# Seven products for the last first product: attention and a two-layer network on one Trainium2 core

## The chip, the cores and the metric

One core of a Trainium2 chip runs the whole program. The metric is the device time of one launch in microseconds (us). The kernel before takes 290.84 us, the median of three runs (290.55 to 291.35).

## The reference

Eight batches of eight heads, 576 tokens, 64 columns a head. Each token attends to the tokens at most 32 places from it. The result, all heads of a token side by side (4608 tokens of 512 columns), goes through two matrix products with the square of ReLU between them.

```python
scores = scale * np.matmul(q, k.transpose(0, 1, 3, 2))
mask = np.abs(pos[:, None] - pos[None, :]) <= window
attn = softmax(np.where(mask, scores, -1e9))
x = np.matmul(attn, v).transpose(0, 2, 1, 3).reshape(B * S, H * D)
h = x @ w_in
r = np.maximum(h, 0.0)
return (r * r) @ w_out
```

`w_in` is 512 x 2048 and `w_out` 2048 x 512. All matrix products take bf16 and add up in f32.

## The kernel before, in words

**Units and groups.** The tokens are counted in units of 64, 72 in all. Attention goes by groups G of 192 tokens (24 of them). For a group: POOL issues the loads of q, k and v, which turn f32 into bf16 on the way (`load_qk`, L469; `load_v`, L517); SP issues DMA transposes of q and k (`turn_dma`, L603; the first six groups are turned on PE by `turn_pe`, L555); PE makes the scores (`S6B` is that of group 6), ACT takes the exponent (`X`), DVE multiplies by the mask (`M`), PE multiplies by v (`P6A`, `P6B`, L753), DVE takes the reciprocal (`R`) and writes the normalised rows into XA and XB (`N`), and SP turns these by DMA into XT (`T6a`, `T6b`, L854 and L857). The first groups (G under NXT) are turned on PE instead, into a bank of `at`, and ACT copies them to XT (L833, L838, L850).

**First product** (`mm1`, L862). `A3840.4` is the product of the tile that starts at token 3840 and of hidden blocks 4 and 5 (128 columns each): four matmuls a block, over the four quarters of 512 columns, into a bank `ht`. ACT takes the ReLU (`r`), ACT or DVE the square (`g`), into the ring GT. Tiles have 192 tokens up to token 2304 and 256 from there (TILES).

**Second product** (`mm2_pair`, L935). Two blocks of 128 tokens (pair u, u + 1) are taken together, as a 2 x 2 block product by seven products instead of eight (Winograd's form of Strassen's): DVE makes four sums S of GT (L951), each of `P1.u` to `P7.u` is eight matmuls of 256 columns on PE (L965), two products to a bank, and ACT and DVE add up the banks: a copy `p1`, the sums `u2`, `u4` and `c22` of 256 columns, `cc` of 512 and a last copy `c11`. The combinations TW of `w_out` are made once (`setup_tw`). The first two blocks go the plain way (`mm2`, `B0.0`). From pair ULATE on, every other pair takes the attention's banks in `at` and other buffers. ACT issues the stores (`st`).

**What sets the order.** Every step is recorded with its engine, what it reads and writes, a planned duration and a key: the place in units at which it is wanted. `schedule` (L168) plays the program through with these numbers and gives each engine, whenever it is free, the ready step with the least key. OFFS moves the keys of ACT's and DVE's steps by kind, FLEX lets some steps go to ACT or DVE, whichever is free, at a handicap, and NOISE moves every key by a draw from SEEDS. What comes out is a fixed order for each engine; each engine then works through its own in turn, and waits on semaphores by bank or buffer. The keys: attention of group G at 3 G - LEAD, a tile of the first product at its place in units, pair u at 2 u + LAGP, so LAGP is the lag of the second product behind the first. Loads wait for a gate: the second v product of the group GD before theirs.

Of the kernel before, what the change touches and what calls it, by code (L numbers as in the profile page):

```python
# [6 lines left out]
ALU = mybir.AluOpType  # L7
# [14 lines left out]
TG = 6  # L22
NXT = 3
# [6 lines left out]
GK = 8.0  # L30
TDKEY = 6
XKEY = (0.2, 0.5)
QMOVE = 14.8
HMOVE = 27
# [5 lines left out]
TGAP = 28  # L40
NVR = 24
VKEY = 10.0
TSLACK = 3500
XSLACK = 2500
LSLACK = 3000
# [19 lines left out]
TILES = ((192, 2304), (256, 4608))  # L65
SEEDS = (54889, 73113, 37345, 76131, 20885, 97248, 47624, 10448, 1997, 7471, 50773, 3305, 47783, 64133, 39018, 28670, 69087, 23028, 92194, 70005)
NOISE = 0.0
NBIAS = 1
PKEY = 2
# [12 lines left out]
LAGP = 8.0  # L82
PSTEP = 0.4
SLEAD = 2.5
MOE = -1
SQBEG = 768
ULATE = 28
HLATE = 4352
E3 = 576
E3B = 1  # L90
OFFS = {'S': 3.25, 'M': -1.5, 'g': 2.25, 'Z': -3.5, 'N': 2.75, 'cc.': -4.25, 'u': -2.75, 'X': 3.25, 'r': -2.25, 'c': -2.25}
DLEAD = 0.3
TWKEY = 6
# [3 lines left out]
FLEX = {'g': 5.25, 'Z': 4.75, 'ev': 3.0, 'o': 6, 'p': 0.75}  # L97
# [259 lines left out]
class Gen:  # L357
# [105 lines left out]

    def gate(self, G):
        if G < 6:
            return None
        return self.p.named[GATE.format(G - GD)] if G >= GFAR else self.moe

    def load_qk(self, t, b, g, key):  # L469
# [6 lines left out]
        for j in range(2):  # L476
            self.p.rec("POOL", lambda e, j=j: e.dma_start(raw[0:h, j, :].rearrange("p (h d) -> p h d", h=8), s[:, j]),  # L477
                       writes=[("raw", t, G % NRAW, j)], dma=(f"{t}{G % NRAW}{j}", G), key=key, dur=500 + 3 * h,
                       move=(h // 2, QMOVE), name=f"{t}{b}{g}{j}", after=self.gate(3 * b + g), slack=LSLACK if b > 1 else 0)
# [22 lines left out]
    def load_pair(self, t, b, g, key):  # L502
# [11 lines left out]
                   reads=[("pr", t, G % NPR)], writes=[("raw", t, G % NRAW, x) for x in range(2)], key=3 * G - LEAD - PKEY if b == 0 else key, dur=430,  # L514
                   name=f"c{t}{b}{g}")

    def load_v(self, b, g, key, js=(0, 1)):  # L517
        G = 3 * b + g
        vt = self.V[G % NV]
        for j in js:  # L520
            k0 = 192 * g - 32 + 128 * j
            lo, hi = max(k0, 0), min(k0 + 128, S_)
            if g and j == 0 and G < NVR:
# [4 lines left out]
                writes=[("v", G % NV, j)], dma=(f"v{G % NV}{j}", G), key=key, dur=500 + 3 * n, move=(n // 2, VMOVE),  # L528
# [89 lines left out]
    def scores(self, G, ws):  # L618
# [3 lines left out]
        key = 3 * G - LEAD + 0.3 * ws[0]  # L622
# [60 lines left out]
    def scores_steps(self, G):  # L683
# [3 lines left out]
        key = 3 * G - LEAD  # L687
# [41 lines left out]
    def pv(self, G, w):  # L729
        b, g = divmod(G, 3)  # L730
        n = 2 * G + w
        key = 3 * G - LEAD + 0.3 * w + 0.1
# [56 lines left out]
    def xturn(self, G):  # L789
        xa, xb = self.XA[G % 3], self.XB[G % 3]  # L790
        key = 3 * G - LEAD + 0.5
        r = 192 * G % RING
        wr = [("xt", (3 * G + c) % (RING // 64)) for c in range(3)]
        if G < NXT:
            ps = self.AT[:, 1024:1536].bitcast(BF16)
            bank = self.half(2)
# [65 lines left out]
    def mm1(self, t0, n, ds, key):  # L862
# [26 lines left out]
        if SQBEG <= t0 < SQEND and k % SQMOD[1] in SQMOD[0]:  # L889
# [6 lines left out]
                   if "g" in FLEX else None)  # L896

# [160 lines left out]
    def build(self):  # L1058
# [40 lines left out]
        for G in range(NG):  # L1099
            b, g = divmod(G, 3)  # L1100
            if b > 1:
                key = 3 * G - LEAD - (GK if G >= GFAR else AHEAD)
# [9 lines left out]
            for ws in ((0,), (1,)) if G < NSPLIT else ():  # L1112
                at(3 * G - LEAD + 0.3 * ws[0], self.scores, G, ws)
# [67 lines left out]
```

## Time and profile before

| | |
|---|---|
| median of the runs | 290.84 us |
| profiled execution, whole | 292.3 us |
| its span, first to last instruction | 290.1 us |
| TensorE's granted clock, mean | 0.999 |
| read from HBM, written | 36.70 MB, 9.44 MB |
| DMA packets | 160645, of which 149984 under 512 B |

The profiled execution spends 2.2 us outside the span and lies 1.5 us above the median. In the tables, PE is TensorE's matmuls, PEld its weight loads, DVE VectorE, ACT ScalarE, POOL GpSimd; a row of a group gives its count, busy time, mean length of one in ns, and the idle time of the engine ahead of it with what ended that. In the stretches, the number after an engine's name is its busy time in that stretch. In the timeline a row has start, length, engine, line and operation. A matmul's recorded length overlaps that of the next one.

### The profile page before, as it was taken

Reading aid. Unit: us, or ns where it says so; the run is one execution under the profiler, and the core shown is the slowest. Engines: PE = TensorE matmul, PEld = TensorE weight load, DVE = VectorE, ACT = ScalarE, POOL = GpSimd, SP = SyncE. Lnnn points to the kernel's source line nnn. Section 1 sums busy time; section 2 is a strip of 40 time slices with the busy share of each in tenths; the row PEclk is TensorE's granted clock in tenths of the full one; section 3 lists DMA queues with packets and bytes.
Section 4 is the critical chain, followed back from the end, with each engine's and each line's share of the span. In section 5 each row is a group of like instructions: output and inputs, shape, how many; then the busy total and the mean of one; then the engine's idle time right before and its main releaser. Section 6 shows DMA issues by size and latency. Waiting matters only on the chain.

```text
span 290.1 us, 8378 instructions
## 1 busy us (share of the span) xinstructions
PE 283.0 (98%) x3426; PEld 245.6 (85%) x3430; DVE 208.2 (72%) x451; ACT 206.3 (71%) x379; POOL 107.0 (37%) x143
## 2 busy tenths in 40 slices
PE   7988999999999999999999999999999999999996
PEld 2467885889999999999998898888888888988885
DVE  6668779878687878686968886766876877735263
ACT  3379987586989988778776677758687638688520
POOL 8986660141566066326415435606236000000000
PEclk9999999999999999999999999999999999999999
DMA  9999999999999999999999999999999921202024
GB/s 161 188 194 186 197 178 139 200 135 173 113 143 209 129 165 119 173 171 143 124 150 189 150 127 169 131 190 90 169 106 139 143 91 29 84 18 76 0 75 145
DMA packets 160645, 39.97 MB, mean 138 GB/s; under 512 B 149984, under 2 KB 156256, under 8 KB 160608
## 3 DMA queue, kind: packets, MB, share of 16 engines
q0 software_dynamic: 106016, 17.93, 94.2%
q1 hardware_dynamic: 49552, 12.47, 31.4%
q10 hardware_dynamic: 5040, 9.05, 9.8%
q8 instruction: 27, 0.44, 0.7%
q14 instruction: 10, 0.08, 0.1%
HBM read 36.70 MB, written 9.44 MB: 159 GB/s over the span
## 4 chain that ended last, share of the span: by engine, by line
PE 87%; DVE 6%; ACT 3%; DMA 1%; issue 1%; ACTq 0%; DVEq 0%
PE ht L879 39%; PE outp L965 29%; PE at L965 4%; PE at L753 4%; PE at L697 3%; PE outp L405 2%; DMA oe<-in_q_dram 1%; PE at L879 1%; PE outp L905 1%; PE outp L879 1%; DVE xa L775 1%; DVE tw L932 1%; ACT qt L596 1%; DVE kt L599 1%; ACT e L674 1%
## 5 line engine op out<-in xcount | busy, mean ns | idle before, releaser
L879 PE MATMUL ht<-xt,w 128*128 128x192 bf16 (+1 forms) x1248 | 135.9, 258 | 0.0
L879 PEld LDWEIGHTS ht<-xt,w 128*128 128x128 bf16 x1248 | 109.3, 98 | 7.9 <-ACT qt L596 0.3
L885 ACT ACTIVATE rt<-ht 128x384 bf16<-128x384 f32 (+1 forms) x156 | 82.4, 534 | 36.4 <-PE ht L879 31.4
L477 POOL DMA_DIRECT2D kraw<-in_k_dram x36 | 27.7, 775 | 113.1 <-PE at L753 54.6
L895 ACT ACTIVATE gt<-rt 128x384 bf16<-128x384 bf16 (+1 forms) x116 | 65.3, 569 | 4.4 <-ACT rt L885 1.5
L526 POOL DMA_DIRECT2D v<-in_v_dram x48 | 37.7, 793 | 0.0
L965 PE MATMUL outp<-w,gt 128*128 128x256 bf16 x240 | 31.1, 273 | 0.0
L965 PE MATMUL outp<-tw,gt 128*128 128x256 bf16 x240 | 31.1, 273 | 0.0
L965 PE MATMUL outp<-tw,ss 128*128 128x256 bf16 x240 | 30.5, 273 | 0.3 <-DVE ss L951 0.2
L893 DVE TENSOR_TENSOR gt<-rt 128x384 bf16<-128x384 bf16 (+1 forms) x52 | 19.9, 386 | 13.5 <-ACT rt L885 13.0
L477 POOL DMA_DIRECT2D qraw<-in_q_dram x36 | 27.7, 773 | 0.0
L711 ACT ACTIVATE e<-at 128x1024 bf16<-128x1024 f32 x21 | 21.4, 1020 | 7.3 <-PE at L697 7.0
L965 PEld LDWEIGHTS outp<-tw,ss 128*128 128x128 bf16 x240 | 22.9, 98 | 3.1 <-issue 0.3
L965 PEld LDWEIGHTS outp<-w,gt 128*128 128x128 bf16 x240 | 23.0, 98 | 3.0 <-ACT oe L915 0.5
L965 PEld LDWEIGHTS outp<-tw,gt 128*128 128x128 bf16 x240 | 22.9, 98 | 2.5
L985 DVE TENSOR_TENSOR oe<-outp,uu 128x256 f32<-128x256 f32 (+1 forms) x30 | 16.6, 554 | 8.2 <-ACT rt L885 4.9
L719 DVE TENSOR_TENSOR pt<-e,mask 128x1024 bf16<-128x1024 bf16 x21 | 14.5, 691 | 11.1 <-ACT e L711 11.0
L753 PE MATMUL at<-v,pt 128*128 128x66 bf16 x384 | 20.1, 194 | 0.1
L753 PEld LDWEIGHTS at<-v,pt 128*128 128x128 bf16 x384 | 17.8, 98 | 2.2 <-ACT at L783 0.4
L725 DVE TENSOR_TENSOR pt<-em,mask 64x512 bf16<-64x512 bf16 x42 | 17.6, 420 | 1.7 <-ACT em L714 0.3
L775 DVE TENSOR_TENSOR xa<-at,rs 64x512 bf16<-64x512 f32 x24 | 16.7, 695 | 1.1
L775 DVE TENSOR_TENSOR xb<-at,rs 128x512 bf16<-128x512 f32 x24 | 16.5, 686 | 0.8
(112 smaller groups left out, 321.8 us busy)
## 6 DMA issues: line engine op xcount, KB each, us to landing
out_dram<-oe ACTq DMA_DIRECT2D x34, 256.0 KB, 4.0
qraw<-in_q_dram POOLq DMA_DIRECT2D x36, 96.0 KB, 6.2
w<-in_moe_w_in_dram POOLq DMA_DIRECT2D x4, 512.0 KB, 11.1
v<-in_v_dram POOLq DMA_DIRECT2D x16, 128.0 KB, 7.8
w<-in_moe_w_out_dram POOLq DMA_DIRECT2D x4, 512.0 KB, 17.7
v<-in_v_dram POOLq DMA_DIRECT2D x16, 96.0 KB, 7.0
kraw<-in_k_dram POOLq DMA_DIRECT2D x12, 112.0 KB, 5.5
kraw<-in_k_dram POOLq DMA_DIRECT2D x12, 96.0 KB, 4.4
```

The costliest lines, as they stand in the source:

```text
L477: self.p.rec("POOL", lambda e, j=j: e.dma_start(raw[0:h, j, :].rearrange("p (h d) -> p h d", h=8), s[:, j]), writes=[("raw", t, G % NRAW, ...
L526: self.p.rec("POOL", lambda e, j=j, lo=lo, hi=hi, k0=k0: e.dma_start(vt[lo - k0:hi - k0, j, :, 0:64], self.v[b, :, lo:hi, :].rearrange("h ...
L711: self.p.rec("ACT", lambda e: e.activation(e2[:], self.AT[:, 0:1024], ACTF.Exp, scale=0.125), reads=lo, writes=[("e", n)], key=key, dur=ac ...
L725: self.p.rec("DVE", lambda e, w=w, r=r, x=x, mm=mm: e.tensor_tensor(pt[x:x + 64, w, :, 0:64], e1[r:r + 64, :].rearrange("p (h q) -> p h q" ...
L753: mm = e.matmul(avp[:, c:c + VS], pt[:, 4 * (h % 2) + h // 2, :], vt[:, w, h, :], start=(w == 0 and y == 0), stop=True, skip_group_check=True)
L775: self.p.rec("DVE", lambda e: e.tensor_tensor(x[r0:128, :].rearrange("p (x y c) -> p x y c", x=2, y=4), av[:, :, :, 0:64], rb, ALU.mult), ...
L879: mm = e.matmul(ht[:, n * x:n * x + n], self.W1[:, ft, 128 * d:128 * d + 128], self.XT[:, ft, r:r + n], start=(ft == 0), stop=(ft == 3))
L885: self.p.rec("ACT", lambda e: e.activation(rt[:, 0:c], ht[:, 0:c], ACTF.Relu), reads=htag, writes=[("rt", k % 4)], key=key, dur=act(c), na ...
L893: self.p.rec("DVE", lambda e: e.tensor_tensor(gt[:, d0:d0 + len(ds), r:r + n], rr, rr, ALU.mult), reads=[("rt", k % 4)], writes=wr, key=ke ...
L895: alt=("ACT", lambda e: e.activation(gt[:, d0:d0 + len(ds), r:r + n], rr, ACTF.Square), act(c), "g")
L965: mm = e.matmul(op[:, 256 * half:256 * half + 256], a[:, d, :], w[:, d, :], start=first and d == 0, stop=d == 7, skip_group_check=True)
L985: self.p.rec("DVE", lambda e: e.tensor_tensor(out, src, other, ALU.add), reads=btags[bank] + rd, writes=wr, key=key + k * PSTEP - DLEAD, d ...
```

## The change

**The first product of the last 512 tokens.** Tokens 4096 to 4607 are one tile (STR1), a 2 x 2 block product by seven products: halves of the hidden width, of the 512 columns, and of the tokens. `setup_w1s` makes four combinations of `w_in` (eight DVE steps of 1024 columns, `ws`) in buffers of q and k that the last groups no longer need. `mm1_tile` makes four differences of XT (`t`, 512 columns each, on DVE). `mm1_pair` is called for dd = 0 to 7 and does hidden blocks dd and dd + 8 for all 512 tokens: four PE steps `a` to `d` of 4, 4, 2 and 4 matmuls of 256 columns into two banks, a copy `p1` and a ReLU of 256 columns on ACT, sums `u2`, `u4`, `c22` (256 columns) and `cc` (512) on DVE, a maximum over 768 columns (DVE or ACT) and a square over 1024 (DVE or ACT). Even dd use the banks `ht`, odd dd two of `at`.

**The numbers.** Tiles of 192 tokens go on to token 3072. NXT goes from 3 to 5, so groups 3 and 4 are turned on PE. Attention's key falls by 0.2 a group from group 6 on (`pos`), so a group takes 2.8 units. The lag of the second product is 9 and grows by 0.2 for each block past the eighth, to 14.2. Loads from group 12 on are gated one group earlier. Planned times of late loads and transposes, OFFS, FLEX, NOISE and SEEDS change, and with them the order of nearly everything.

```diff
-NXT = 3
+NXT = 5
-GK = 8.0
+GK = 7.0
+LAGS = 0.2
+GDL = 1
-TSLACK = 3500
-XSLACK = 2500
-LSLACK = 3000
+TSLACK = 2200
+XSLACK = 3000
+LSLACK = 2000
+STR1 = (4096,)
+LG0 = 6
+LGS = 0.2
+WLEAD = 5.0
-TILES = ((192, 2304), (256, 4608))
+TILES = ((192, 3072), (256, 4608))
-NOISE = 0.0
+NOISE = 0.4
-LAGP = 8.0
+LAGP = 9
-SLEAD = 2.5
+SLEAD = 1.0
-ULATE = 28
-HLATE = 4352
+ULATE = 26
+HLATE = 3840
...
+    def pos(self, G):
+        return 3 * G - LEAD - max(0, G - LG0) * LGS
...
-        return self.p.named[GATE.format(G - GD)] if G >= GFAR else self.moe
+        return self.p.named[GATE.format(G - GD - GDL * (G > LG0))] if G >= GFAR else self.moe
...
+    def mm1_pair(self, t0, dd, key):
...
+        banks = [(self.HT[0][:], self.HT[1][:]), (self.AT[:, 1024:1536], self.AT[:, 1536:2048])][i]
...
+        L = [w(0, lo), w(1, lo), ws(3), w(1, hi), ws(0), ws(1), ws(2)]
+        R = [B[0, 0], B[1, 0], B[1, 1], T[3], T[0], T[1], T[2]]
...
+        prod((0, 5), 0, (0, 1), True, 0, "a")
+        prod((4, 6), 1, (0, 1), True, 1, "b")
...
+        add(u2, al[:, 256:512], p1, btags[0] + tp1[:1], tu2, 1, 256, f"u2.{t0}.{dd}")
+        add(u4, be[:, 0:256], u2, btags[1] + tu2[:1], tu4, 2, 256, f"u4.{t0}.{dd}")
+        add(rh[:, 768:1024], be[:, 256:512], u4, btags[1] + tu4[:1], rtag[2], 3, 256, f"c22.{t0}.{dd}")
+        prod((1,), 0, (0,), False, 4, "c")
...
+        prod((2, 3), 1, (0, 1), False, 5, "d")
...
-            key = 2 * u + LAGP - 4 * (u == NBLK - 2)
+            key = 2 * u + LAGP + LAGS * max(0, u - 8) - 4 * (u == NBLK - 2)
```

**The order, at two places.** First PE around the start of the second product, some 45 to 55 us into the run. In the kernel before, from the last parts of B1 and B0 (L905) to P1, P5 and P7 of pair 2 (L965) and the first tile past 576 tokens (L879):

```order
L905 MATMUL outp<-w,gt 128x512 x4
L753 MATMUL at<-v,pt 128x66 x8
L905 MATMUL outp<-w,gt 128x512 x4
L965 MATMUL outp<-w,gt 128x256 x8
L965 MATMUL outp<-tw,ss 128x256 x8
L965 MATMUL outp<-tw,gt 128x256 x8
L879 MATMUL ht<-xt,w 128x192 x16
```

In the changed kernel the same place, where L891 is the first product, L1025 `B`, L1085 `P`, L765 the v product of group 4, and L845 and L850 its turn on PE:

```order
L891 MATMUL ht<-xt,w 128x192 x16
L765 MATMUL at<-v,pt 128x66 x8
L1025 MATMUL outp<-w,gt 128x512 x4
L891 MATMUL ht<-xt,w 128x192 x16
L1025 MATMUL outp<-w,gt 128x512 x4
L765 MATMUL at<-v,pt 128x66 x8
L1025 MATMUL outp<-w,gt 128x512 x8
L1085 MATMUL outp<-w,gt 128x256 x8
L845 MATMUL at<-ident,xa 128x64 x4
L850 MATMUL at<-ident,xb 128x128 x4
L1085 MATMUL outp<-tw,ss 128x256 x16
```

The eight steps of tile 576 (A576) moved from behind P1 of pair 2 to ahead of it, and the turn of group 4 came in.

Then the end of the tile of seven products. On PE of the changed kernel (L968 is `mm1_pair`): P6, P5 and P7 of pair 30, the two operands of A4096.7d, P2, P3 and P4 of pair 30, and P1 of pairs 32 and 34:

```order
L1085 MATMUL at<-tw,qraw 128x256 x16
L1085 MATMUL at<-tw,gt 128x256 x8
L968 MATMUL at<-xt,kraw 128x256 x2
L968 MATMUL at<-qt,w 128x256 x2
L1085 MATMUL at<-w,gt 128x256 x8
L1085 MATMUL at<-w,qraw 128x256 x8
L1085 MATMUL at<-tw,gt 128x256 x8
L1085 MATMUL outp<-w,gt 128x256 x8
L1085 MATMUL at<-w,gt 128x256 x8
```

On DVE of the changed kernel, the same place: c22.4096.7 (into v3), u2.30, the square of dd = 6, cc.4096.7, u4.30 and c22.30, then the first S of pairs 34 and 32 (L1071):

```order
L995 TENSOR_TENSOR v3<-at,v1 128x256
L1105 TENSOR_TENSOR e1<-at,e0 128x256
L1014 TENSOR_TENSOR gt<-v2 128x2x512
L995 TENSOR_TENSOR v3<-at,v0 128x512
L1105 TENSOR_TENSOR em0<-at,e1 128x256
L1105 TENSOR_TENSOR oe<-at,em0 128x256
L1071 TENSOR_TENSOR qraw0<-gt 128x1024
L1071 TENSOR_TENSOR ss<-gt 128x1024
```

In the kernel before, A4352.14, the last step of its first product, has the fourteen products of pairs 32 and 34 behind it; here A4096.7d, the last of the new one, has three products of pair 30 and these fourteen behind it, and u4.30 and c22.30 stand behind cc.4096.7 on DVE.

More of the change, by code (lines that the diff above doesn't have):

```diff
@@ L29 @@
 GD = 3
-GK = 8.0
-TDKEY = 6
+GK = 7.0
+TDKEY = 5.0
 XKEY = (0.2, 0.5)
 QMOVE = 14.8
+QM2 = 21.4
+TBK = 0
+LAGS = 0.2
+KPL = 0
+GDL = 1
 HMOVE = 27
@@ L794, in xturn @@
         if G < NXT:
-            ps = self.AT[:, 1024:1536].bitcast(BF16)
-            bank = self.half(2)
+            ps = (self.OUTP[0][:] if 0 < G < TBK else self.AT[:, 1024:1536]).bitcast(BF16)
+            bank = ["outp0"] if 0 < G < TBK else self.half(2)
             two = G < NBIAS
```

141 lines of the change are left out of this document (120 added, 21 removed), and 4 rows, old and new, of the table OPENING.

## Prediction

> **What bounds the kernel now.** First the page, for the span, the busy shares and the chain that ended last.
>
> ```profile
> span 290.1 us, 8378 instructions
> PE 283.0 (98%) x3426; PEld 245.6 (85%) x3430; DVE 208.2 (72%) x451; ACT 206.3 (71%) x379; POOL 107.0 (37%) x143
> PE 87%; DVE 6%; ACT 3%; DMA 1%; issue 1%; ACTq 0%; DVEq 0%
> ```
>
> The chain of work that ended last runs through PE for 87%. The page does not say where the other 13% lies, so next comes the busy time of each engine by stretches, cut where the work changes.
>
> ```profile
> core 0: us, PE busy (x) PEld busy (x) DVE busy (x) ACT busy (x) POOL busy (x), PEclk, DMA share, GB/s
> 0.00:20.00 20.00, 17.34 (x148) 8.89 (x150) 13.17 (x47) 8.98 (x12) 17.67 (x27) 1.00 1.35 179
> 20.00:40.00 20.00, 18.95 (x288) 17.44 (x288) 15.24 (x33) 19.65 (x40) 12.56 (x17) 1.00 1.64 188
> 40.00:75.00 35.00, 34.48 (x430) 27.98 (x430) 29.43 (x62) 25.25 (x49) 11.16 (x16) 1.00 1.78 160
> 75.00:196.00 121.00, 120.92 (x1582) 110.45 (x1581) 91.77 (x190) 93.73 (x181) 51.79 (x68) 1.00 1.71 154
> 196.00:260.00 64.00, 64.00 (x740) 56.56 (x738) 45.01 (x96) 46.08 (x79) 13.84 (x18) 1.00 0.92 98
> 260.00:287.40 27.40, 27.34 (x251) 24.26 (x248) 13.19 (x25) 12.58 (x23) 0.00 (x0) 1.00 0.16 59
> ```
>
> From 75 us to 287.4 us PE is never idle, at a granted clock of 1.00, while DVE and ACT leave a fifth to a half of their time. There only the sum of PE's own work can shorten the kernel. Before 40 us ACT is full (19.65 of 20 us), so work put on ACT there is paid for. After 260 us DVE has 14 us to spare and ACT 15 us: this is the cover that the change draws on.
>
> A busy sum counts pipelined matmuls more than once, so PE's work is priced from start to start. These are two steps of the chain in order of time (16 matmuls of 192 tokens, 16 of 256) and the group of one product by shape.
>
> ```profile
> 130.86 1.32 PE ht L879 x16
> 257.64 1.75 PE ht L879 x16
> L965 PE MATMUL outp<-w,gt 128*128 128x256 bf16 x240 | 31.1, 273 | 0.0
> ```
>
> A matmul of 256 columns takes 1.75/16 = 0.109 us of PE, one of 192 takes 0.0825 us; a product of eight takes 0.87 us. The group's own mean, 273 ns, is two and a half times that. [...] By the mean, 16 matmuls fewer would be 4.4 us; by the steps, which I use, 1.75 us.
>
> **The change part by part.** *PE's own work.* The first product of the last 512 tokens took 16 hidden blocks x 4 x 2 = 128 matmuls of 256 columns and takes 7 products x 2 x 8 = 112: -16 x 0.109 = -1.75 us. Then NXT sends the turns of groups 3 and 4 to PE. PE's rows where group 1 is turned price that:
>
> ```profile
> 26.58 0.29 PE L833 MATMUL at<-ident,xa 64*128 64x64 bf16 x4 [0.61 <-DVE xb L775]
> 26.80 0.40 PE L838 MATMUL at<-ident,xb 128*128 128x128 bf16 x4
> 27.03 0.82 PE L879 MATMUL ht<-xt,w 128*128 128x192 bf16 x8
> ```
>
> From 26.58 to 27.03 is 0.45 us a group: +0.90 us. TILES takes 768 tokens from tiles of 256 to tiles of 192: 256 x 0.0825 - 192 x 0.109 = 21.1 - 20.9 = +0.2 us. PE's sum: -1.75 + 0.90 + 0.2 = -0.65 us. No other edit touches the number of matmuls.
>
> *The waits of PE that the new order can take away.* PE's rows between 45 and 75 us show two, each with a neighbour that starts on time:
>
> ```profile
> 50.91 1.05 PE L965 MATMUL outp<-w,gt 128*128 128x256 bf16 x8
> 52.05 1.03 PE L965 MATMUL outp<-tw,ss 128*128 128x256 bf16 x8
> 62.51 0.42 PE L753 MATMUL at<-v,pt 128*128 128x66 bf16 x8
> 62.76 1.03 PE L965 MATMUL outp<-tw,gt 128*128 128x256 bf16 x8
> 64.64 0.41 PE L753 MATMUL at<-v,pt 128*128 128x66 bf16 x8
> 65.28 1.05 PE L965 MATMUL outp<-tw,ss 128*128 128x256 bf16 x8 [0.22 <-DVE ss L951]
> ```
>
> P1 of pair 2 takes 1.14 us to the next start instead of 0.87 (DVE is still making TW), and the step at 64.64 takes 0.64 us where the one at 62.51 takes 0.25 (S of pair 4 is late): 0.27 + 0.39 = 0.66 us. In the new order a whole tile of 192 tokens (A576, eight groups of 0.66 us) comes ahead of P1 of pair 2, and pair 4 starts a tile later. I take both waits as gone, -0.65 us; the bounds are 0 and, if the 0.61 us wait in the row at 26.58 goes as well, -1.3 us. That one I expect to stay: the turn of group 1 still stands behind the same mask, reciprocal and XB on DVE. What comes next where these go is PE's queue itself.
>
> *ACT before 45 us.* XT of groups 3 and 4 adds two evictions on ACT, and two of K's evictions move there from DVE, against two squares and a clearing that move off; from 20 to 40 us there is no cover. By the rows below (0.81 us an XT) the bounds are 0 and +1.0 us; I take 0, since the XTs come after 40 us, where ACT has 10 of 35 us free, and what is added and removed before that differs by less than one of them. With the turns go four transposes of SP's queue; at that place no wait of PE is for one of them, so nothing is gained.
>
> *The last stretch, DVE.* These are groups by shape: DVE's reads of 256 and 512 columns of PSUM, S, square, copy, then ACT's.
>
> ```profile
> L985 DVE TENSOR_TENSOR uu<-outp,uu 128x256 f32<-128x256 f32 x30 | 12.6, 421 | 3.1 <-ACT uu L976 1.5 <-PE outp L965 0.5
> L985 DVE TENSOR_TENSOR oe<-outp,uu 128x512 f32<-128x512 f32 x15 | 10.4, 691 | 8.0 <-ACT rt L885 4.9 <-PE outp L965 2.9
> L951 DVE TENSOR_TENSOR ss<-gt 128x1024 bf16<-128x1024 bf16 x15 | 10.3, 689 | 3.0 <-ACT gt L895 2.4 <-PE outp L965 0.2
> L893 DVE TENSOR_TENSOR gt<-rt 128x512 bf16<-128x512 bf16 x24 | 10.1, 424 | 7.6 <-ACT rt L885 7.3
> L512 DVE COPY qraw<-tw 96x1024 bf16<-96x1024 bf16 x5 | 2.4, 472 | 0.1
> L711 ACT ACTIVATE e<-at 128x1024 bf16<-128x1024 f32 x21 | 21.4, 1020 | 7.3 <-PE at L697 7.0
> L850 ACT ACTIVATE xt<-at 128x768 bf16<-128x768 bf16 x2 | 1.6, 811 | 0.1
> ```
>
> From A4096.0a to the end of A4096.7d PE has 112 x 0.109 + 15 products x 0.87 = 25.3 us of work. DVE's queue over the same stretch (u2.26 to cc.4096.7) holds 31 sums of 256 columns, 10 of 512, 3 S, 3 squares of 1024 and 2 maxima: 31 x 0.42 + 10 x 0.69 + 6 x 0.69 + 2 x 0.47 = 25.0 us. The maximum over 768 columns of bf16 has no row; the copy of 1024 (0.47) is nearest, bounds 0.42 and 0.69. [...] Either way DVE, which had up to half its time free here, is as full as PE, and what it has left over for waiting is 0.3 us. Its four t and eight ws (1.7 and 5.5 us) come earlier, the ws spread over the middle of the run, where a quarter of DVE is free: nothing.
>
> Where that shows is the end of the stretch. How long DVE takes to see a product:
>
> ```profile
> 270.58 1.04 PE L965 MATMUL at<-w,gt 128*128 128x256 bf16 x8
> 271.66 0.42 DVE L978 COPY oe<-at 128x256 f32<-128x256 f32 x1 [0.79 <-PE at L965]
> ```
>
> 270.58 + 0.87 is 271.45, and DVE starts 0.2 us later. With T the end of A4096.7d: cc.4096.7 ends at T + 0.2 + 0.69, u4.30 and c22.30 behind it in DVE's queue end at T + 1.73. P3.30 needs c22.30; PE has only P2.30 (0.87 us) until then, and waits 0.86 us. Nothing had to wait there before. The square of the last pair (0.81 + 1.02 us on ACT after cc) ends at T + 2.72, ahead of P1.32 at T + 3.5, and the S of pairs 32 and 34 fit beside the 14 products left: no second wait. I take +0.86 us, bounds +0.6 us (each of the three sums starts some 0.1 us before the one ahead has ended) and +3.0 us (the hand-offs between ACT, DVE and PE inside the eight units add two more waits of 1 us, since DVE cannot catch up).
>
> *Loads.* These are PE's scores of groups 6, 10 and 23, then the turns of XB (time to landing, and one issue of them) and the PE step that needs that one:
>
> ```profile
> 67.13 0.23 PE L697 MATMUL at<-qt,kt 64*128 64x64 bf16 x4
> 103.28 0.41 PE L697 MATMUL at<-qt,kt 64*128 64x64 bf16 x16
> 244.28 0.41 PE L697 MATMUL at<-qt,kt 64*128 64x64 bf16 x16
> DMA to landing us min/median/max: 2.4/6.3/8.3
> 84.00 2.03 SPq L857 DMA_TRANSPOSE xt<-xb  x1
> 94.83 1.43 PE ht L879 x16
> ```
>
> A group comes every 9.0 us at first (36.2/4) and every 10.8 us after (141/13). The new keys put 2.8 units between groups instead of 3, which is about 10.1 us: loads and turns come closer, but not closer than they stood early on, where the turn issued at 84.00 lands by 92.3 at the longest, 2.5 us ahead of its reader. At the end T23b has 13 products (11.3 us) between P23B and A4096.0a; reciprocal, u2, XB, turn and t take 0.2 + 0.2 + 0.42 + 0.69 + 6.3 + 0.42 = 8.2 us. I take 0, bounds 0 and +2 us.
>
> *Sum*: -0.65 - 0.65 + 0.86 = -0.44 us. The profiled execution took 292.3 us, 2.2 us outside its span of 290.1; nothing outside the span is changed. It lies 1.5 us over the median of 290.84, so the difference goes to the median: **290.4 us**. A measurement of this kernel tells 0.3%, 0.87 us, from no change.
>
> **The rivals.** *DVE sets the last 40 us (slower).* The eight units pass each sum from ACT to DVE to PE, one bank at a time. For it: 25.0 of 25.3 us, and every wait of DVE stays. Against it: sums that do not depend on each other start before the one ahead has ended, so 25.0 is high. With waits of 3.0 us, 290.84 - 1.30 + 3.0 = 292.5 us; from 2.2 us on the kernel is slower by over 0.3%. [...] Chance 0.15.
>
> *A turn lands late (slower).* XT of one group comes after its first product is due, and PE, in order, waits. For it: denser groups, and two turns of K and Q between XA and XB in SP's queue. Against it: the margin of 2.5 us at 9 us a group, and loads gated one group earlier. A turn 4 us later than the longest here costs 4 - 2.5 = 1.5 us: 291.9 us; it decides from 3.8 us on. Chance 0.08.
>
> *The small early waits go too (faster).* PE stood idle for 20 - 18.95 = 1.05 us from 20 to 40 us (0.61 of it in the row at 26.58) and for 0.5 us from 40 to 75; the whole order is drawn anew there, with a larger lag and so with more first products at hand when something is late. Against it: ACT is full from 20 to 40 us and gets no less to do. 290.4 - 1.05 = 289.35 us; with the other 0.5 us 288.9. Chance 0.30.
>
> *The gain is not made (no change).* XT and K on ACT before 45 us take what the order gives: 290.84 - 0.65 + 0.86 = 291.05 us or some tenths less. Chance 0.07.
>
> **How the numbers follow.** The forecast case (289.8 to 291.0) has 0.40; 0.07 of it lies under 289.97. Faster: 0.30 + 0.07 = 0.37. Same: 0.33 + 0.07 = 0.40. Slower: 0.15 + 0.08 = 0.23. The range runs from 288.6 (the faster rival's 288.9 less the 0.26 us between the last wait and its lower bound) to 292.3 (nearly all of DVE's case), and leaves out some 0.15.
>
> **What would show it.** Right: 112 matmuls of the seven products at 0.109 us; no PE step over 0.9 us at P1 of pair 2 or of pair 4; one PE wait for DVE's c22 near P3.30 of 0.8 to 1.3 us; DVE over 90% busy in the stretch from A4096.0a; no wait named DMA. Wrong: PE idle by over 2 us after 245 us, PE waits between 20 and 45 us that grew by over 0.5 us, or a wait for xt, kt or qt.

## The result, and the profile after

The changed kernel takes 292.94 us, the median of six runs (292.06 to 293.86), against 290.50 us for the kernel before (six runs, 290.20 to 291.35): ratio 1.0073, 95% interval 1.0052 to 1.0094, slower by 2.4 us. The forecast was 290.4 us with a range to 292.3; it failed on the side of slower. (Ratios here leave out an execution over 1.5% above the fastest of its kernel; medians don't.)

The page of the changed kernel, where the prediction showed those of before: span and instructions, busy times, the chain that ended last.

```profile
span 290.5 us, 8608 instructions
PE 280.7 (97%) x3488; PEld 246.5 (85%) x3494; DVE 222.8 (77%) x488; ACT 213.2 (73%) x404; POOL 107.0 (37%) x143
PE 85%; ACT 7%; DVE 3%; DMA 2%; issue 1%; SPq 0%; DVEq 0%
```

PE's busy time fell by 2.3 us and the kernel became longer: PE now stands idle where it didn't. The stretches of the changed kernel after 75 us, with the columns as before:

```profile
75.00:196.00 121.00, 119.39 (x1654) 110.90 (x1653) 94.59 (x201) 100.01 (x201) 60.67 (x79) 1.00 1.86 161
...
260.00:287.40 27.40, 26.61 (x243) 23.39 (x241) 20.00 (x43) 11.73 (x22) 0.00 (x0) 1.00 0.15 54
```

Before, PE was busy for 120.92 of the 121 us from 75 to 196; now it misses 1.6 us there, where the change was thought to do nothing, and 0.8 us at the end. The view of waits names them (what waited, for what; us in total, times, longest; first PE's, then one of DVE's):

```profile
PE ht L891 <- ACT rt L897: 0.9, 2, 0.8
PE at L709 <- DVE xb L787: 0.8, 1, 0.8
PE at L1085 <- DVE oe L1105: 0.8, 1, 0.8
...
DVE kraw L924 <- DMA kt<-kraw: 2.6, 2, 1.9
```

Only the third was forecast. The timeline of the changed kernel at the first one: scores of group 8 on PE, the last step of A960 and the first of A1152 (16 matmuls), ACT's two exponents of group 8, the two ReLUs behind them, and A1152.2.

```profile
83.10 0.52 PE L709 MATMUL at<-qt,kt 64*128 64x64 bf16 x24
83.56 1.50 PE L891 MATMUL ht<-xt,w 128*128 128x192 bf16 x16
83.87 0.59 ACT L726 ACTIVATE em<-at 128x512 bf16<-128x512 f32 x1
84.34 1.03 ACT L723 ACTIVATE e<-at 128x1024 bf16<-128x1024 f32 x1
85.25 0.88 ACT L897 ACTIVATE rt<-ht 128x384 bf16<-128x384 f32 x2
85.81 0.83 PE L891 MATMUL ht<-xt,w 128*128 128x192 bf16 x8 [0.75 <-ACT rt L897]
```

The last matmul of A960.14 is recorded to 84.39, just after ACT has begun the exponent of 1024 columns (84.34). Its ReLU has to wait until 85.25, and A1152.2, which wants that bank, starts at 85.81, 0.92 us late from start to start. The second wait, at the scores of group 19. The rows are N of group 18 (first half), a weight sum (`ws10`, L924), reciprocal and N of its second half, then the scores:

```profile
182.34 0.69 DVE L787 TENSOR_TENSOR xa<-at,rs 64x512 bf16<-64x512 f32 x1
185.61 0.69 DVE L924 TENSOR_TENSOR kraw<-kraw,w 128x1024 bf16<-128x1024 bf16 x1 [1.89 <-DMA kt<-kraw]
186.65 0.21 DVE L784 RECIPROCAL rs<-at 128x8 f32<-128x8 f32 x1
186.97 0.69 DVE L787 TENSOR_TENSOR xb<-at,rs 128x512 bf16<-128x512 f32 x1
187.71 0.52 PE L709 MATMUL at<-qt,kt 64*128 64x64 bf16 x24 [0.82 <-DVE xb L787]
```

The weight sum is not needed for another 60 us. But it writes into a buffer of K whose DMA transpose has not landed, so DVE, in order, stands for 1.89 us, and XB of group 18 behind it. The third, at the end (A4096.7d, cc.4096.7, u4.30, c22.30, P3.30):

```profile
271.54 0.38 PE L968 MATMUL at<-qt,w 128*128 128x256 bf16 x2
271.96 0.69 DVE L995 TENSOR_TENSOR v<-at,v 128x512 bf16<-128x512 f32 x1 [0.34 <-PE at L968]
272.57 0.41 DVE L1105 TENSOR_TENSOR em<-at,e 128x256 f32<-128x256 f32 x1
273.08 0.42 DVE L1105 TENSOR_TENSOR oe<-at,em 128x256 f32<-128x256 f32 x1
273.57 1.05 PE L1085 MATMUL at<-w,qraw 128*128 128x256 bf16 x8 [0.77 <-DVE oe L1105]
```

To add all this up I took, for every step of PE, the time to the start of the next step, less what a step of its kind takes where nothing waits (0.66 us for eight matmuls of 192, 0.87 for eight of 256, and so on): that is waiting. What is left from the first product A0.0 to the last matmul is PE's own work. The stretches are counted from A0.0; `b_again` is a second trace of the kernel before, told of below.

```
            A0.0  own work  waits | 0-57  57-133  133-178  178-228  228-end
b_again    17.55    262.33   5.40 | 3.67    0.73     0.43     0.57     0.01
changed    17.72    261.62   8.21 | 3.01    2.31     1.30     0.43     1.16
a_late     17.73    261.62   7.37 | 3.05    2.31     0.51     0.33     1.16
a_all      17.79    261.62   6.29 | 2.94    2.12     0.52     0.33     0.38
a_16       17.74    263.38   6.25 | 3.04    2.34     0.42     0.43     0.02
b_7        17.14    260.57  16.75 | 4.23    0.74     0.52     0.44    10.82
b_lag      17.21    262.33   7.22 | 4.15    1.44     1.09     0.53     0.01
```

The changed kernel: own work -0.71, waits +2.81, start +0.17, in sum 2.27 us; counted this way PE's last matmul ends at 287.55 us instead of 285.29.

### The profile page after: what moved, and what is told of

Read it like the earlier page. It is cut to its first block, busy times and chain, and to the rows that moved or that the text cites. A ratio compares the mean times of both kernels' runs of the same rounds, so it can differ in the third digit from the quotient of the medians.

```text
span 290.5 us, 8608 instructions
## 1 busy us (share of the span) xinstructions
PE 280.7 (97%) x3488; PEld 246.5 (85%) x3494; DVE 222.8 (77%) x488; ACT 213.2 (73%) x404; POOL 107.0 (37%) x143
## 4 chain that ended last, share of the span: by engine, by line
PE 85%; ACT 7%; DVE 3%; DMA 2%; issue 1%; SPq 0%; DVEq 0%
PE ht L891 32%; PE outp L1085 30%; PE at L1085 6%; PE at L765 4%; PE at L709 3%; ACT rt L897 2%; PE at L968 2%; PE ht L968 2%; DMA oe<-in_k_dram 2%; PE outp L1025 1%; PE outp L891 1%; PE at L891 1%; ACT e L686 1%; ACT gt L907 1%; ACT kt L613 1%
## 5 line engine op out<-in xcount | busy, mean ns | idle before, releaser
L891 PE MATMUL ht<-xt,w 128*128 128x192 bf16 (+1 forms) x1184 | 120.7, 251 | 1.1 <-ACT rt L897 0.9
L891 PEld LDWEIGHTS ht<-xt,w 128*128 128x128 bf16 x1184 | 99.3, 98 | 6.5 <-ACT rt L897 1.7
L897 ACT ACTIVATE rt<-ht 128x384 bf16<-128x384 f32 (+1 forms) x148 | 73.6, 511 | 21.7 <-PE ht L891 15.9
L907 ACT ACTIVATE gt<-rt 128x384 bf16<-128x384 bf16 (+1 forms) x107 | 58.6, 554 | 3.0 <-ACT rt L897 0.3
L1085 PE MATMUL outp<-tw,gt 128*128 128x256 bf16 x224 | 29.1, 273 | 0.0
L1085 PE MATMUL outp<-w,gt 128*128 128x256 bf16 x224 | 29.0, 273 | 0.0
L1085 PE MATMUL outp<-tw,ss 128*128 128x256 bf16 x224 | 28.5, 273 | 0.0
L905 DVE TENSOR_TENSOR gt<-rt 128x384 bf16<-128x384 bf16 (+1 forms) x53 | 19.1, 363 | 10.8 <-ACT rt L897 10.1
L1085 PEld LDWEIGHTS outp<-w,gt 128*128 128x128 bf16 x224 | 21.5, 98 | 2.5
L1085 PEld LDWEIGHTS outp<-tw,ss 128*128 128x128 bf16 x224 | 21.7, 98 | 2.2
L1085 PEld LDWEIGHTS outp<-tw,gt 128*128 128x128 bf16 x224 | 21.4, 98 | 2.4
L765 PE MATMUL at<-v,pt 128*128 128x66 bf16 x384 | 20.1, 194 | 0.1
L765 PEld LDWEIGHTS at<-v,pt 128*128 128x128 bf16 x384 | 17.8, 98 | 1.8 <-ACT pt L683 0.3
```

The costliest lines, as they stand in the source:

```text
L765: mm = e.matmul(avp[:, c:c + VS], pt[:, 4 * (h % 2) + h // 2, :], vt[:, w, h, :], start=(w == 0 and y == 0), stop=True, skip_group_check=True)
L891: mm = e.matmul(ht[:, n * x:n * x + n], self.W1[:, ft, 128 * d:128 * d + 128], self.XT[:, ft, r:r + n], start=(ft == 0), stop=(ft == 3))
L897: self.p.rec("ACT", lambda e: e.activation(rt[:, 0:c], ht[:, 0:c], ACTF.Relu), reads=htag, writes=[("rt", k % 4)], key=key, dur=act(c), na ...
L905: self.p.rec("DVE", lambda e: e.tensor_tensor(gt[:, d0:d0 + len(ds), r:r + n], rr, rr, ALU.mult), reads=[("rt", k % 4)], writes=wr, key=ke ...
L907: alt=("ACT", lambda e: e.activation(gt[:, d0:d0 + len(ds), r:r + n], rr, ACTF.Square), act(c), "g")
L1085: mm = e.matmul(op[:, 256 * half:256 * half + 256], a[:, d, :], w[:, d, :], start=first and d == 0, stop=d == 7, skip_group_check=True)
```

## The experiments

Unless said otherwise, an experiment keeps the order of the changed kernel and moves single instructions in it. A few lines at the end of the program do that, once the planner is through; waits are worked out anew from what each instruction reads and writes:

```python
for x, rel, y in MOVES:
    o.remove(n[x])
    o.insert(o.index(n[y]) + (rel == "after"), n[x])
```

**The kernel before, once more (`b_again`).** No edit.

> The kernel before, once more, for a second trace. Theory: its first profiled execution started late (first product A0.0 at 19.18 us, 290.1 us of span, against a median that asks for 288.2 to 288.6): here A0.0 lies at 17.4 to 18.0 us, and PE's waits after 20 us are those of the first trace. Rival: 19.2 us is the usual start of this order, and the changed kernel's 17.72 us is a gain of the change.

Measured: 290.45 us, span 288.3 us. The first product in the first trace of before, in this one, and in `a_light` (below):

```profile
19.18 0.83 PE L879 MATMUL ht<-xt,w 128*128 128x192 bf16 x8
```

```profile
17.55 1.13 PE L879 MATMUL ht<-xt,w 128*128 128x192 bf16 x9
```

```profile
19.61 0.82 PE L891 MATMUL ht<-xt,w 128*128 128x192 bf16 x8
```

The late start belongs to single executions, of either kernel, and costs 1.6 to 1.9 us. The first trace of before was one of them. Laid side by side, the two first traces (290.1 and 290.5 us of span) show 0.4 us of a loss of 2.4.

**One weight sum later (`a_ws`).**

```diff
+MOVES = (('ws10', 'after', 'g3072.10'),)
```

> The changed kernel with one instruction moved in DVE's order: the third of the eight weight sums (ws10, 1024 columns) goes from its place between the XA of group 18 and the V copy of group 19 to a place eleven us later, behind the squares of A3072.10. Theory W (the loss is a handful of single waits that this one order holds): DVE no longer stands 1.89 us behind the transpose of K, XB of group 18 comes in time, PE's wait of 0.98 us ahead of the scores of group 19 goes, and nothing else is late: 292.94 - 0.98 = 291.95 us, ratio to the kernel before 1.005. Theory D (the denser order leaves DVE and ACT without room, a wait that is taken away comes back at a later hand-over): 292.7 to 293.0 us, with a new PE wait between 188 and 204 us.

Measured: 291.97 us median of nine runs (291.84 to 299.3), ratio 1.0065 (1.0040 to 1.0089). Its profiled execution took 297.41 us. In its trace the wait at group 19 is gone, and another stands 14 us earlier: the transpose of K of group 18, the first weight sum (`ws00`), and the product of group 17 with V, whose mask stood behind it on DVE.

```profile
161.85 1.34 SPq L620 DMA_TRANSPOSE kt<-kraw  x1
...
171.92 0.69 DVE L924 TENSOR_TENSOR kraw<-w 128x1024 bf16<-128x1024 bf16 x1 [3.24 <-DMA kt<-kraw]
...
173.72 0.60 PE L765 MATMUL at<-v,pt 128*128 128x66 bf16 x8 [2.14 <-DVE pt L737]
```

The median is Theory W's to 0.02 us. But three of nine executions lie 2.9 to 7.3 us above it. The trace is of one of them (297.41) and shows why for that one: another weight sum has the same weakness. The other two have no trace. This transpose took 9.9 us to land here, 7.8 in the first trace of the changed kernel, 9.5 in `a_three`, 7.2 in `a_relu`.

**All weight sums later (`a_late`).**

```diff
+MOVES = (('ws00', 'before', 'M18m0'), ('ws01', 'before', 'R20A'), ('ws10', 'before', 'S1.22'), ('ws20', 'before', 'S4.24'),
+         ('ws11', 'before', 'R23A'), ('ws30', 'before', 'g3840.4'), ('ws21', 'before', 'S4.28'), ('ws31', 'before', 'S4.28'))
```

> The changed kernel with all eight weight sums (ws00 to ws31) moved later in DVE's order, each into a place where DVE stood idle by 0.7 us or more, at least 5 us behind the usual landing of the transposes that they wait for (ws00 from 166 to 177 us, ws01 to 200, ws10 to 205, ws20 to 226, ws11 to 230, the last three to 238 to 241). Theory J (DVE stands behind transposes of K and Q whose landing moves by microseconds from execution to execution, and with it stand the masks and XB): the 0.98 us at the scores of group 19 go, and so do the larger losses of some executions: median 291.8 us, ratio 1.004, the executions within 1.0 us of each other. Theory W (one wait of one order, the rest as in the profile): 292.0 us with the same spread as the changed kernel's (1.8 us and more). Theory D (DVE has no room): 292.7 us or more.

Measured: 292.02 us median of twelve (291.74 to 294.36; ten of them within 0.6 us), ratio 1.0040 (1.0018 to 1.0062). Between W and J: 0.9 us is gone (the interval still meets that of the changed kernel) and no weight sum waits for a DMA in the trace, though the transposes of Q and K landed no sooner there (median 7.2 us, 6.4 in the changed kernel's trace). The median is the one that W gave. The spread fits neither: two of twelve lie 1.5 and 2.3 us above the median, where J said 1.0 us for all, and the kernel before, run beside it, spread by 2.3 us too (290.18 to 292.49). What speaks for J is that none of twelve is over 294.4 us, where three of nine of `a_ws` were over 294.8. So few executions don't settle it.

**A ReLU to DVE (`a_relu`).** The ReLU is written a second time as a maximum for DVE.

```diff
+MOVES = (('r960.14', 'before', 'M8m1'), ('A1152.4', 'before', 'P8A'))
+TO_DVE = ('r960.14',)
```

> The changed kernel with the ReLU of A960.14 (384 columns) put from ACT, where it stands behind the two exponentials of group 8, on DVE ahead of the masks of group 8, and A1152.4 ahead of the products of group 8 with V on PE. Theory W: PE's wait of 0.92 us at A1152.2 falls to some 0.2 us, since the bank is free 0.8 us earlier: 292.94 - 0.7 = 292.2 us, ratio 1.006. Theory D: the masks of group 8, now 0.5 us later, hold the products with V as long: 292.8 to 293.0 us.

Measured: 291.98 us median of eleven (291.11 to 296.24), ratio 1.0043 (1.0028 to 1.0059). But the trace does not put that gain here. The 0.92 us behind A1152.0 became 0.16, 0.08, 0.23 and 0.18 behind the next steps: from 57 to 133 us PE's waits fell from 2.31 to 2.13 us. The rest is `ws10`, whose transpose had landed in time in this trace. At this place Theory D held: ACT is full (11.2 of 12 us busy from 78 to 90 us in the changed kernel), and the wait that was taken away came back in pieces.

**The end (`a_tail`).**

```diff
+MOVES = (('A4096.7d', 'before', 'P7.30'), ('g4096.6', 'after', 'c22.30'))
```

> The changed kernel with two instructions moved: on PE the last product of the seven (A4096.7d) goes ahead of P7.30 instead of behind it, on DVE the square of A4096.6 goes behind c22.30. Theory W: the 0.94 us that PE waits at P3.30 is only the queue of DVE (the 512-column sum of A4096.7d ahead of u4.30 and c22.30); with one product more between that sum and P3.30 the wait falls to 0.2 to 0.35 us: 292.94 - 0.6 to 0.7 = 292.3 us, ratio 1.006. Theory D: DVE is full from A4096.0a on, so the wait stays or comes back at P1.32: 292.9 to 293.2 us.

Measured: 292.50 us median of six (292.03 to 292.98), ratio 1.0070 (1.0054 to 1.0087). The wait at P3.30 did fall to 0.34 us, and P1.32 got one of 0.45. ACT's rows of `a_tail`, the copy c11.30, the maximum and the square of A4096.7, and P1.32:

```profile
272.62 0.38 ACT L1096 ACTIVATE oe<-at 128x256 f32<-128x256 f32 x1 [1.67 <-PE at L1085]
272.90 0.83 ACT L1010 ACTIVATE v<-v 128x768 bf16<-128x768 bf16 x1
273.77 1.06 ACT L1016 ACTIVATE gt<-v 128x1024 bf16<-128x1024 bf16 x1
...
274.97 1.03 PE L1085 MATMUL outp<-w,gt 128*128 128x256 bf16 x8 [0.29 <-ACT gt L1016]
```

The maximum had its data at 271.74, the end of cc.4096.7, and stood behind a copy that waited for P2.30. I had looked at DVE's queue and not at ACT's.

**The three moves together (`a_three`).** The edits of `a_ws`, `a_tail` and `a_relu`.

> The changed kernel with the moves of the last three runs together. Theory W: the three waits are terms of one sum, PE has no wait of over 0.5 us left after 75 us: 292.94 - 0.98 - 0.65 - 0.7 = 290.6 us, ratio 1.000 to 1.001. Theory D: 292.4 to 293.0 us, the waits stand elsewhere.

Measured: 292.05 us median of nine (291.04 to 299.97), ratio 1.0047 (1.0025 to 1.0070). Between the theories, with a `ws00` that stood 2.27 us behind its transpose in the trace. This run and `a_ws` led to Theory J.

**All mended (`a_all`).** The edits of `a_late`, `a_relu` and `a_tail`, and one more:

```diff
+        ('r4096.7', 'before', 'c11.30'),
```

> The last run's moves, those of a_relu, and those of a_tail with one more: on ACT the maximum of A4096.7 goes ahead of the copy c11.30, behind which it stood in a_tail. Theory J with W: 291.8 - 0.7 (A1152.2) - 0.6 (P3.30) = 290.5 us, ratio 1.000, executions within 1.0 us. Theory D: 291.5 us or more, the waits stand elsewhere.

Measured: 290.96 us median of twelve (290.55 to 292.69), ratio 1.0012 (0.9991 to 1.0033). The time is 0.5 us over the forecast and the executions spread by 2.1 us, not 1.0. P3.30's wait is 0.34 us and P1.32's is gone. Thirteen instructions put elsewhere, of 8608, took back 2.0 us: most of the loss of the change was in its order. Of the waits from 57 to 133 us nearly all are still there (2.12 us of 2.31). It ties with the kernel before; no version tried beats it.

**Without the seven products (`a_16`).** The order is planned anew, and is that of the changed kernel up to about 165 us.

```diff
-STR1 = (4096,)
+STR1 = ()
```

> The changed kernel without the seven products (STR1 empty: 16 units of 8 products for the last 512 tokens as before; the order is drawn anew with all its other numbers). Theory J: PE's work grows by 1.75 us, the waits at P3.30 (0.94) and behind the weight sums (0.98 and more in some executions) go: 292.94 + 1.75 - 0.94 - 0.98 = 292.8 us, give or take 0.7 us for the new order, and the executions lie within 1.0 us. Rival P (the seven products themselves are the loss, the rest of the change is neutral): 290.5 us, the time of the kernel before.

Measured: 293.52 us median of six (293.40 to 293.57), ratio 1.0089 (1.0066 to 1.0113). PE's own work is 263.38 us, 1.76 us more than with the seven products. That is the upper edge of the forecast. Rival P is out: the rest of the change is not neutral. Without the seven products it loses 3.0 us, by the table 1.05 us of PE's own work and 0.85 us of waits; another 0.85 us lies behind PE's last matmul. That tail also makes the seven products look better than they are. The changed kernel is 0.6 us faster than `a_16`, but its last matmul ends 0.2 us later (287.55 against 287.37): its new waits eat the 1.76 us of work saved. Against `a_late`, which has no harm from weight sums, the seven products gain 1.5 us, of which 0.65 us at PE's last matmul and 0.9 us in the tail. The six runs of `a_16` lie within 0.2 us.

**The seven products alone (`b_7`).** The changed program with every other number as in before.

> The kernel before with the seven products alone: the changed program with all numbers of before (NXT, the tiles of 192 and 256 tokens, lags, keys, seeds); up to 180 us the order is that of before, behind that the planner puts the weight sums and the seven products in. Theory J with W: PE's work -1.75 us, a wait of about 0.9 us at the last A4096.7d, and 0 to 1.0 us behind weight sums that wait for transposes: 290.45 - 1.75 + 0.9 = 289.6 us, up to 290.6; ratio 0.997 to 1.000. Theory D (DVE sets the last 40 us, whatever stands before them): 291.0 us or more.

Measured: 298.91 us median of six (298.09 to 300.91), ratio 1.0294 (1.0263 to 1.0324). The stretch of the eight units in `b_7`, and P1.32 with its wait:

```profile
259.10:276.40 17.30, 14.09 (x118) 10.27 (x116) 15.61 (x37) 12.14 (x24) 0.00 (x0) 1.00 0.09 32
```

```profile
279.44 1.86 PE L1085 MATMUL outp<-w,gt 128*128 128x256 bf16 x8 [2.91 <-ACT gt L1016]
```

Theory D's time, by far: with a lag of 8 units hardly a second product is left to stand between the eight units; they follow each other, and DVE is busy for 15.61 of 17.30 us. PE loses 10.8 us from there on: 4.2 us in waits for DVE's sums, 3.1 us ahead of P1.32, which waits for ACT's square of the last pair, some 2.9 us behind that wait, where the granted clock is 0.50 and eight matmuls of 256 columns take 1.66 us (279.44 to 281.10) instead of 0.87 (an estimate: half of PE's 5.76 us there, last section), and the rest in small pieces. This is the prediction's slower rival, at a price of 10 us instead of 3. In the changed kernel the larger lag holds fifteen products back for this stretch, and there it does not happen. That the lag alone makes this difference is worked out, not shown: no run has the seven products and the lag without the other numbers.

**The lag alone (`b_lag`).** Numbers of before, eight products, the order as before up to about 48 us.

```diff
-LAGP = 8.0
+LAGP = 9
+LAGS = 0.2
```

> The kernel before with the lag alone: LAGP 9 and LAGS 0.2 (second product 9 to 14 units behind instead of 8), eight products for the last 512 tokens, all other numbers those of before; the order is the same up to about 48 us. Theory: a larger lag adds no work; PE's sum is as before, and the time is 290.45 us give or take 0.5 us for the waits of the new order, which stand where first products follow each other with no second product between. Rival L (the lag itself is the loss: more rows of GT in use and units bunched): 291.5 us or more, with PE waits for ACT's ReLU of over 1 us in sum.

Measured: 292.53 us median of six (292.33 to 294.56), ratio 1.0080 (1.0052 to 1.0107). Rival L's time, not its mechanism: work as before (262.33 us) and waits +1.8 us, but of 0.3 to 0.6 us each at several places, two of them (0.7 us) for ACT's copies of the second product and none named for a ReLU; some 0.4 us more go to a load of `w_in` in the opening. Another 0.7 us lies behind the last matmul (3.7 us to the end of the span instead of 3.0): cc and c11 of the last pair come one after the other on DVE, where before c11's product stood last. `a_16` has that tail too. So a larger lag alone loses 2 us in this planner's hands; why its small waits come is not settled.

**A product into the gap (`a_fill`).** `a_all` without the edit of `a_relu`, and instead:

```diff
+        ('P4.4', 'after', 'A1152.0'), ('cc.4', 'after', 'M8A'), ('st4.0', 'after', 'g1152.2'), ('st5.0', 'after', 'st4.0'),
```

> The changed kernel with the weight sums late (as in a_late), the end mended (as in a_all), and instead of the ReLU on DVE one product of pair 4, P4.4, moved on PE from ahead of the scores of group 7 to behind A1152.0; its sum cc.4 and its two stores move behind it on DVE and ACT. Theory F (from 78 to 90 us the new order has no second product left between the first products of A960 and A1152, so ACT, with ReLU, squares and exponentials, sets the pace there, 11.2 of 12 us): the product fills PE's wait of 0.92 us at A1152.2 and what follows comes 0.7 us earlier: 0.5 us less than a_all, 290.5 us, ratio 0.999. Rival: the products with V and the scores behind P4.4 don't come earlier, since DVE's masks set them: as a_late with the end mended, 291.2 us.

Measured: 295.27 us median of six (291.62 to 297.22), ratio 1.0134 (1.0091 to 1.0177). The trace is of the execution of 297.22 us, which also started late. At the place itself it worked: P4.4 and A1152.2 of `a_fill` follow each other, and no wait is left there.

```profile
85.86 1.04 PE L1085 MATMUL outp<-tw,gt 128*128 128x256 bf16 x8
86.78 0.83 PE L891 MATMUL ht<-xt,w 128*128 128x192 bf16 x8
...
171.79 0.53 PE L709 MATMUL at<-qt,kt 64*128 64x64 bf16 x24 [1.77 <-DMA qt<-qraw]
```

But from 103 us on scores wait for transposes of Q and K, as in the last row. Of the move only two stores touch the DMA engines.

**Those two stores alone (`a_st`).** `a_all`, and:

```diff
+        ('st4.0', 'after', 'g1152.2'), ('st5.0', 'after', 'st4.0'),
```

> The moves of a_all, and the two stores of pair 4 (256 KB each) issued on ACT's queue at 88 us instead of 77 us, as they were in a_fill; P4.4 and everything else stay where a_all has them. Theory Q (the DMA engines are the tight resource: 9 tenths busy in nearly every slice up to 225 us; a store that comes while the loads of a group wait puts all loads and transposes behind it late, and the backlog does not clear): loads on POOL's queue after 88 us land 10 us and more behind their issue instead of 6, PE waits for transposes of Q and K, and the time is 293 to 297 us as in a_fill. Rival: the stores cost nothing, a_fill lost by P4.4 itself; then 291.0 us as a_all.

Measured: 296.26 us median of four; too few for an interval. Two have a granted clock of 1.000 and take 293.02 and 294.37 us, two have 0.994 and 0.993 and take 298.37 and 298.15 us; no run of `a_all` is over 292.69. Theory Q, from the trace of the 294.37 us: of PE's waits, 3.3 us more than in `a_all` lie between 129 and 157 us, and three of them end within 0.1 us of the landing of a transpose of Q or XT. Another, 0.8 us, is for ACT's ReLU, and the longest, 1.07 us, has no cause that the profile shows. DMA issues of `a_all` and of `a_st` (count, KB each, median us from issue to landing):

```profile
qraw<-in_q_dram POOLq DMA_DIRECT2D x36, 96.0 KB, 6.1
kt<-kraw SPq DMA_TRANSPOSE x36, 6.5
```

```profile
qraw<-in_q_dram POOLq DMA_DIRECT2D x36, 96.0 KB, 12.6
kt<-kraw SPq DMA_TRANSPOSE x36, 8.0
```

Two stores of 256 KB, issued 10 us later (at 87 us instead of 77), double the landing time of the loads for the rest of the run: those of Q issued from 87 us on took 10 to 18 us, in `a_all` 4 to 8. The page shows how little room there was. The busy tenths of the DMA engines, 40 slices, first of before, then of the changed kernel:

```profile
DMA  9999999999999999999999999999999921202024
```

```profile
DMA  9999999999799999999999999999831222020214
```

Before, they are busy for nine tenths or more until 232 us; in the changed kernel, with nearly the same bytes (39.6 MB for 40.0), until 203. Its only breath is the slice from 73 to 80 us (seven tenths), and the two stores were issued in it, at 77 us; at 87 us they met the loads of the next groups, and the backlog did not clear: in `a_st` that slice is at four tenths, and those behind it stay at nine until 219 us. Loads (POOL's queue, Q's median 6.1 to 12.6 us) and transposes (SP's, K's median 6.5 to 8.0 us) both land later, though the stores are on ACT's queue; how they hold each other up, no run shows.

**Fewer bytes in the same order (`a_light`).**

```diff
-            o = self.OEB[:, v % 4, c0:c1]
+            n1 = c0 + 128 if v < 26 else c1; o = self.OEB[:, v % 4, c0:n1]
```

> The changed kernel in its own order with less to store: of the output rows of tokens 256 to 3327 only 128 of the 512 columns are written (it leaves out 4.7 MB of 40 MB of DMA; nothing else changes). Theory Q: transposes and loads land sooner, the weight sums no longer hold DVE, so PE's wait at the scores of group 19 goes and the executions come closer together: 291.9 to 292.1 us, all within 0.7 us, transposes from 110 to 160 us with a median of 6.3 us to landing or less instead of 6.9. Rival (landing times have nothing to do with the load of the DMA engines): 292.9 us with the spread of the changed kernel.

Measured: 291.93 us median of twelve (291.34 to 294.94; ten of them within 2.1 us), ratio 1.0053 (1.0025 to 1.0081). The median is the one that Theory Q gave, one microsecond less without a single instruction moved, but the interval overlaps that of the changed kernel (from 1.0052), and the spread did not narrow: late starts, like the profiled one, are part of it. In its trace no weight sum waits, and the transposes issued from 110 to 160 us land after a median of 5.4 us instead of 6.9. One trace does not prove that the bytes did it. In `a_tail`, with all its bytes, the same median is 5.6 us, and in `a_relu` no weight sum waits either. This run fits Theory Q; `a_st` is the one that shows it.

## Why the prediction was wrong

What failed are terms that the prediction put at nothing: new waits in the middle of the run (+1.58 us from 57 to 133 us after A0.0) and weight sums that wait for transposes (+0.87 us). The terms that it worked out came close.

*PE's own work: right.* -0.65 forecast, -0.71 measured (262.33 to 261.62). The seven products save 1.76 us (`a_16`, and `b_7` against before) where 1.75 was worked out.

*The early waits and ACT before 45 us: right in sum, in part by luck.* In the first 57 us after A0.0 the waits fell from 3.67 to 3.01 us: -0.66 for -0.65. P1 of pair 2 and P5B are free of theirs, and the wait at the turn of group 1 stayed. But ACT's new work is not free. An eviction of K that DVE had done (20.38 us) now holds the scores behind it on PE (from the view of waits):

```profile
PE at L661 <- ACT kt L613: 0.3, 1, 0.3
```

From start to start those scores are 0.47 us late, 0.20 before. Another new wait, 0.34 us at 51.45 us, is for a ReLU that stood behind evictions of K and Q on ACT. A wait of 0.41 us for XT at 33.8 us, which no step had named, went and made up for much of this.

*The end: right in kind, a little short.* 0.94 us ahead of P3.30, as worked out, and 0.18 behind P3.28, against 0.86. DVE's queue from u2.26 to cc.4096.7 adds up to 24.65 us (25.0 forecast). The maximum over 768 columns is shorter than the row that I took:

```profile
L1008 DVE TENSOR_SCALAR v<-v 128x768 bf16<-128x768 bf16 x2 | 0.7, 351 | 0.0
```

0.35 us against 0.47. "DVE over 90% busy" was wrong: sums overlap (above, cc.4096.7 ends at 272.65 and u4.30 starts at 272.57), and it is 21.59 of 25.55 us.

```profile
246.25:271.80 25.55, 25.54 (x235) 22.66 (x233) 21.59 (x50) 14.86 (x30) 0.00 (x0) 1.00 0.14 52
```

*"Its four t and eight ws ... nothing": the step that failed first.* It reckoned DVE's time, 5.5 us in a stretch with a quarter of DVE free. What a weight sum costs is not its 0.69 us but its place in an order: it waits for a transpose, and masks and XB stand behind it. +0.87 us in the trace from 133 to 178 us after A0.0; `a_late` takes back 0.9 us of the median. The prediction had named the sign, a wait for kt; it came on DVE.

*"Loads. I take 0": failed with it.* It took the old readers one by one (scores, XB's turn), with a margin of 2.5 us, and asked neither which new readers there are nor how full the DMA engines were. The same 72 transposes of Q and K are issued within 164 us (46.6 to 210.2) instead of 180 (48.8 to 229.1), and the time to landing grew (us, minimum, median, maximum; before, then changed):

```profile
DMA to landing us min/median/max: 2.4/5.2/9.1
```

```profile
DMA to landing us min/median/max: 2.4/6.4/9.6
```

The rival "a turn lands late" (0.08) had the right cause with another reader.

*What was in no step: +1.58 us from 57 to 133 us.* The new order does pair 4 and P1 of pair 6 ahead of A960; then the first twelve of the sixteen steps of A960 and A1152 follow with only attention between them (77.4 to 88.0 us), and ACT, 11.2 of 12 us busy from 78 to 90, sets the pace. Before, P3.4, P4.4, P1.6 and P5.6 stood between those steps, and ACT had nearly as much to do (10.65 of 12 us) without holding PE. `a_fill` shows that one product there takes the 0.92 us away. The rest of the 1.58 us is in small pieces that no run took apart. I showed two places of the new order; this was a third. The prediction's "the order is drawn anew" was used only as a hope (the faster rival, 0.30).

*The sum.* Forecast -0.65 - 0.65 + 0.86 = -0.44. Measured by the same terms: -0.71 - 0.66 + 1.15 = -0.22 us. Unforeseen: +1.58 + 0.87, and -0.14 from 178 to 228 us. With the start's +0.17 this makes 2.26 us at PE's end, of 2.44 us between the medians. The base of the forecast, 290.84 us, was 0.34 us above the later median, which made the miss look smaller. The slower cases got 0.23 and the range ended at 292.3, because the working gave every engine's free time away as cover and looked for new waits only where the change was drawn.

## What to carry to other kernels

Where every engine works through a fixed order, an instruction put into another engine's free time costs what it waits for, not what it takes (here `ws10` takes 0.69 us and stood for 1.89): look up what it waits for, and who stands behind it. The DMA engines, at nine tenths and more until 203 us but for one slice, had no time to spare here: two stores issued 10 us later took the median landing of Q's loads from 6.1 to 12.6 us, so a new time of a store is a change of its own. A new reader of a transfer there wants a margin of the spread of its landing (here 3 us, from 7.0 to 9.9 for one transpose). Before two traces are laid side by side, compare their first useful instruction: a late start can be nearly as large as the effect (here 1.6 to 1.9 us, of 2.4).

## What the runs showed of the hardware

- In two traces a wait of PE was paid for twice: the granted clock fell to 0.50 at it, and the matmuls behind it took longer. In `a_ws` a wait of 2.14 us ended at 173.72, and from 173.78 on the clock was 0.50 for 3.41 us (16 matmuls of 192 took 2.55 us, not 1.32). In `b_7` it fell at 278.38, 1.85 us into a wait of 2.91 us, and stayed there for 6.83 us. After a wait of 1.77 us (`a_fill`, ended at 171.79) it was 1.00 from 172 to 176, and in the changed kernel it is 1.00 for the 2.8 us behind the last matmul as well (287.72 to 290.5). What makes it fall, and for how long, these traces don't show. In the execution of 297.41 us of `a_ws`, wait, half clock and late start make 2.1 + 1.7 + 1.6 = 5.4 us, which is what it lies over the median. First `a_ws`, then `b_7`:

```profile
173.78:177.19 3.41, 3.41 (x27) 3.16 (x28) 2.56 (x6) 0.77 (x2) 0.00 (x0) 0.50 1.82 154
278.38:285.21 6.83, 5.76 (x28) 4.01 (x29) 4.90 (x8) 0.92 (x1) 0.00 (x0) 0.50 0.00 0
```

- With the DMA engines at nine tenths and more, one and the same transpose (K of group 18) took 7.0 (`a_tail`) to 9.9 us (`a_ws`) to land in different executions, 5.8 us in `a_light` with fewer bytes, and two stores of 256 KB at a worse time doubled the landing of 96 KB loads (6.1 to 12.6 us) for 100 us and more.
- Some executions start 1.6 to 1.9 us late (A0.0 at 19.2 to 19.6 instead of 17.1 to 17.9 us), of either kernel; why was not tried.
